# Second last chunk's first MLP products shared between token halves, and the last chunk's inverse placed by VectorE transposes

## The chip, the core and the metric

The kernel runs on one NeuronCore of a Trainium2 chip. The metric is the device time of one execution in microseconds (us). The core has a matrix engine (TensorE, PE in the profile; its weight loads are PEld), a vector engine (VectorE, DVE), an engine for functions and copies (ScalarE, ACT), a general engine (GpSimd, POOL) and a queue that issues most of the transfers (SyncE, SP). Each engine runs its own instructions in the order in which they were written down and waits on semaphores for the others. Products land in PSUM, eight banks of 128 partitions x 512 numbers; everything else lies in SBUF.

## The reference

```python
B, H, S, D = 4, 8, 768, 48                # q, k, v; beta is (B, H, S)
k_n = k / (norm(k) + 1e-6)
state = zeros(B, H, D, D)
for t in range(S):                        # the attention block
    y[:, :, t] = q_t @ state
    v_old = state^T @ k_n_t
    state = state + beta_t * outer(k_n_t, v_t - v_old)
x = y with heads side by side             # 3072 tokens x 384
h = x @ w_in                              # w_in 384 x 2048
out = (h * sigmoid(h)) @ w_out            # w_out 2048 x 384
```

## The kernel before

The sequence of 768 steps is cut into six chunks of 128 (`c` = 0 to 5), each with two halves of 64 steps. With four batches a half has 256 tokens for the MLP.

**Attention.** The recurrence inside a chunk is solved with the inverse of a triangular matrix. For each chunk `prepare` makes the scores of keys and queries (L539), sends the 32 x 32 diagonal blocks to DRAM and back (`block_out`, `block_in`), and `invert` builds their inverse on VectorE: 31 pairs of a rank-one product (L656) and an add (L661), then a scaling (L664). From chunk 2 on the inverse goes from there to DRAM and back (`low`, `up`, `read_up`) to reach the partitions at which the two `merge` steps (L808) want it; chunk 1 instead calls `put_up`, which makes two 32 x 32 block transposes on VectorE and ten copies (six by ScalarE, two by VectorE, two by GpSimd). `solve(c)` then has the merges, the products with keys, values and queries (L854, L866, L886, L932, L945), and for each half the copies of the output into `xT` (L554), part of them by way of DMAs (L925).

**MLP.** The 2048 features are 16 blocks of 128, worked through as eight pairs. For chunks 0 to 4 `hidden(c, hf)` does one half at a time: a pair takes 2 x 3 products of 128 x 256 into one bank `phid` (two banks, called M, in turn), and ScalarE applies `silu` (L1098) into `gT`. For the last chunk `hidden_of_both` (products at L1303) takes both halves at once. It treats two neighbouring pairs as a 2 x 2 block matrix (two feature blocks by two of the three 128-row blocks of `w_in`) times a 2 x 2 block matrix (those rows by two halves) and makes that with seven block products in place of eight; the third block of rows is added plainly. So a group of two pairs takes 22 products in place of 24. The price is sums of blocks of `w_in` and of `xT` (four each, VectorE), copies of intermediate values by ScalarE, and adds by VectorE (L1277). The steps of a group are `first` (6 products), `second` (the rest). `combine(c, hf)` makes the second MLP product in the same manner: 7 x 8 products of 192 columns (L1200) into the banks `px` and `py`, with sums of `gT` on VectorE (L1183) and the results collected in `o` and `kept`.

**Order.** TensorE gets these parts interleaved by hand. A string for each chunk says what comes next: `s` a step of `solve`, `r` the next three or four products of the MLP, `y` a step of `prepare`, `g` the start of an inverse, `i` one pair of its rank steps, `m` norms for a later chunk. Every instruction is pinned behind the one before it on its engine (`pin`), so that the string fixes the order on each of them. PSUM banks are dealt out by name: M (two), A (three), CC (three). A bank is taken again when the last reader of its old content is done.

```python
def bank(room, name):
    tag = room[0]
    room.rotate(-1)
    return kept_banks.get(tag) or banks.tile([P, 512], FP32, name=name, tag=tag)
...
for c in range(1, NCH):
    if c > 1:
        solving = solve(c)
        if c < LAST: pieces = chained(pieces, feed_forward(c, 0), feed_forward(c, 1))
        else:        pieces = chained(pieces, hidden_of_both(c), combine(c, 0), combine(c, 1))
    ready = prepare(c + 1)
    for word in chunks[c].split(): ...
```

Of the kernel before, what the change touches and what calls it, by code (L numbers as in the profile page):

```python
# [19 lines left out]
def kernel(  # L20
# [374 lines left out]
    def norm_steps(c):  # L395
# [25 lines left out]
        if c < 2:  # L421
# [24 lines left out]
    def place(c, j):  # L446

        return 2 * (1 - j % 2) + j // 2 if c > 1 else j
# [181 lines left out]
    def put_up(x):  # L630

        both = work.tile([P, BH, T], FP32, name="xe_y", tag="g", bufs=1)
        xes[1], ys[1] = both[:], both[:].rearrange("p (g h) t -> p g h t", g=2)
        pin(nc.vector.transpose(out=both[:].rearrange("p n s -> p s n"), in_=x))
        up = work.tile([P, BH, T], FP32, name="up_1", tag="x", bufs=1)[:]
        pin(nc.vector.transpose(out=up.rearrange("p n t -> p t n"), in_=x.rearrange("p s t -> p t s")))
        for j in (1, 3, 0, 2):
# [7 lines left out]
    def invert(c, step):  # L645
# [23 lines left out]
        if c == 1:  # L669
            put_up(x)  # L670
# [390 lines left out]

    def hidden_rows(c, hf, fs):

        if (c, hf) in ((0, 1), (LAST, 0)):
            return kq_rows[:, fs]
        if c == LAST:
            i, n = fs.start // (NFF // 4), fs.start % (NFF // 4)
            room = kbufs[i][:].rearrange("p b a e w -> p (b a e w)").rearrange("p (f t) -> p f t", t=2 * GT)
        else:
            room, n = gTs[fs.start // FG], fs.start % FG  # L1070
        return room[:, n : n + fs.stop - fs.start]
# [4 lines left out]
    def groups_of(c):  # L1076

        n = NFF // 4 if c == LAST else FG
        return [slice(f, min(f + n, NFF // 2)) for f in range(0, NFF // 2, n)]

    def hidden(c, hf):

        for f in range(NFF // 2):
            assert ("in", f) in narrowed
            ph = bank(M, "phid")
            for j in range(2):
                for a in range(NKT):
                    pin(nc.tensor.matmul(  # L1088
                        ph[:, j * GT : (j + 1) * GT],
                        lhsT=w_in[:, a, (2 * f + j) * P : (2 * f + j + 1) * P],  # L1090
                        rhs=xTs[c, hf][:, a, :],
                        start=(a == 0), stop=(a == NKT - 1),
                    ))
                if j == 0:
                    yield
            if f % FG == 0 and (c, hf) != (0, 1):
                gTs[f // FG] = mlp.tile([P, FG, 2 * GT], FP32, name="gT", bufs=3)
            pin(nc.scalar.activation(  # L1098
                out=hidden_of(c, hf, f), in_=ph[:], func=ACTF.Silu, scale=-0.5 if in_blocks(c) else 0.5
            ))  # L1100
# [74 lines left out]
    def sum_g(c, hf, which, g):  # L1175
        k, left, right, op = which
        fs = groups_of(c)[g]
# [7 lines left out]
    def combine(c, hf):  # L1185
# [27 lines left out]
        def steps(chain, *halfway):  # L1213
# [7 lines left out]
        gs = range(len(groups_of(c)))  # L1221
        yield from steps(
            chain(px[:, left], (0, 0), (0, 0), True), *((s, g) for g in (gs if last else gs[-1:]) for s in (S1, S2))
# [36 lines left out]

    def hidden_of_both(c):

        free = deque((*M, *CC, *A))
        sums = stage[:, 0 : 3 * NFF // 2 * P].rearrange("p (k f m) -> p k f m", k=3, m=P)
        turns = stage[:, 3 * NFF // 2 * P :].rearrange("p (k t) -> p k t", k=4)

        def of_w(i, k, fs):
            return w_in[:, k].rearrange("p (f i m) -> p f i m", i=2, m=P)[:, fs, i]

        def left(which, fs):  # L1270
            return of_w(*which, fs) if isinstance(which, tuple) else sums[:, which - 1, fs] if which < 4 else of_w(1, 0, fs)

        def right(which):
# [523 lines left out]
```

## Time and profile before

| | |
|---|---|
| median of 3 runs | 632.37 us (631.95 to 634.43) |
| the profiled execution, its own time | 633.96 us |
| its span, first to last instruction | 631.8 us |
| TensorE busy | 617.7 us, 98% of the span |
| VectorE busy | 415.5 us, 66% |
| ScalarE busy | 226.7 us, 36% |
| GpSimd busy | 94.0 us, 15% |
| granted clock of TensorE, mean | 0.989 |

The time of an execution is its span and some 2 us around it. A row of the timeline has the start in us from the span's start, the length, the engine, the line of the kernel, the operation, what it writes and reads, the shapes, and in brackets how long the engine stood idle before and what ended that. Rows of equal instructions are merged (`x12`). The chain of work lists the pieces that ended last, in order of time, with start, length and count; there a product of 128 columns of weights counts twice, since it has two records in the trace.

### The profile page before, as it was taken

To read this page: it belongs to the slowest core of one execution; us is meant where nothing else is said; L and a number is where in the kernel's file an instruction comes from. 1 tells how busy PE (TensorE), PEld (TensorE's weight loads), DVE (VectorE), ACT (ScalarE), POOL (GpSimd) and SP (SyncE) were. 2 spreads that over 40 slices of the span, in tenths; PEclk is the share of its full clock that TensorE was granted. 3 is DMA by queue.
4 is the path that set the end of the run, shared out by engine and by line. 5 is a ranking of instruction groups with operands and counts; after the bars stand their busy time and mean duration, and the time that the engine had idled before them with its cause. 6 is when DMAs were issued, how large, how long until landed. Compare 5 with 4: busy or idle time off the path is not lost.

```text
span 631.8 us, 21374 instructions
## 1 busy us (share of the span) xinstructions
PE 617.7 (98%) x9390; PEld 543.3 (86%) x9390; DVE 415.5 (66%) x927; ACT 226.7 (36%) x516; POOL 94.0 (15%) x101
## 2 busy tenths in 40 slices
PE   8889989999999999999999999999999999999997
PEld 5578778666799989989989989989989989988997
DVE  6886779999667974546975554976444983345432
ACT  4657873332441122451122451122452122454210
POOL 5234631335020020020020010020002000000000
PEclk9869999999999999999999999999999999999999
DMA  9656506350459360459141359433254024010011
GB/s 175 134 141 199 170 16 149 116 86 4 101 100 186 62 108 4 95 107 188 34 92 20 72 125 156 65 75 44 52 113 95 2 75 62 17 38 1 0 26 26
DMA packets 136941, 52.61 MB, mean 83 GB/s; under 512 B 108672, under 2 KB 130432, under 8 KB 136848
## 3 DMA queue, kind: packets, MB, share of 16 engines
q1 hardware_dynamic: 136512, 51.09, 39.6%
q8 instruction: 74, 1.21, 0.9%
q10 hardware_dynamic: 336, 0.15, 0.1%
q14 instruction: 19, 0.16, 0.1%
HBM read 39.09 MB, written 9.96 MB: 78 GB/s over the span
## 4 chain that ended last, share of the span: by engine, by line
PE 93%; SPq 2%; DMA 1%; issue 1%; ACT 1%; DVE 0%
PE phid L1088 34%; PE px L1200 17%; PE py L1200 13%; PE po L1132 5%; PE pb_c L866 3%; PE pa L539 2%; SPq L144 2%; PE pb_c L1303 2%; PE pb_c L854 2%; PE pyc L945 2%; PE pc L1303 2%; PE pb_c L1132 2%; PE pb_c L886 2%; PE pa L1303 1%; PE pyc L932 1%; PE px L808 1%
## 5 line engine op out<-in xcount | busy, mean ns | idle before, releaser
L1088 PE MATMUL phid<-xT,w_in 128*128 128x256 f32 x960 | 214.9, 382 | 1.9 <-issue 1.7
L1088 PEld LDWEIGHTS phid<-xT,w_in 128*128 128x128 f32 x960 | 180.2, 190 | 26.9 <-issue 2.8
L1098 ACT ACTIVATE gT<-phid 128x512 f32<-128x512 f32 x72 | 42.9, 597 | 115.2 <-PE phid L1088 106.2
L656 DVE SCALAR_TENSOR_TENSOR rank<-g,step,x 128x31 f32<-128x31 f32 (+15 forms) x124 | 49.8, 402 | 23.3 <-DMA g<-blocks 19.8
L1200 PE MATMUL px<-sums_of_w,sums_of_g 128*128 128x192 f32 x320 | 56.6, 329 | 0.0
L1200 PE MATMUL py<-w_out,sums_of_g 128*128 128x192 f32 x320 | 56.2, 328 | 0.0
L1200 PEld LDWEIGHTS px<-sums_of_w,sums_of_g 128*128 128x128 f32 x320 | 52.2, 190 | 0.4
L1200 PEld LDWEIGHTS py<-w_out,sums_of_g 128*128 128x128 f32 x320 | 52.3, 190 | 0.3
L661 DVE TENSOR_TENSOR x<-x,rank 128x31 f32<-128x31 f32 (+15 forms) x124 | 42.5, 342 | 4.3
L477 POOL TENSOR_TENSOR vf<-vf,n_slot 128x768 f32<-128x768 f32 x10 | 14.8, 1492 | 175.4 <-DMA vf<-in_v_dram 129.9
L1183 DVE TENSOR_TENSOR sums_of_g<-gT 128x384 f32<-128x384 f32 (+1 forms) x48 | 24.6, 540 | 14.6 <-ACT gT L1098 14.5
L498 DVE STREAM_TRANSPOSE kq<-stage 128x512 f32<-128x512 f32 x28 | 28.4, 1121 | 6.8 <-DMA stage<-in_q_dram 3.5
L554 ACT COPY xT<-pyc 48x128 f32<-48x128 f32 (+2 forms) x120 | 31.1, 259 | 1.6
L1211 DVE TENSOR_TENSOR o<-o,kept 128x192 f32<-128x192 f32 (+1 forms) x29 | 11.5, 425 | 26.7 <-ACT kept L1208 26.7
L560 POOL COPY g<-x 64x256 f32<-64x256 f32 x4 | 5.0, 1244 | 150.8 <-DVE x L664 150.8
L891 DVE TENSOR_TENSOR state<-state,pb_c 128x384 f32<-128x384 f32 x22 | 11.2, 550 | 24.6 <-PE pb_c L886 24.6
L866 PEld LDWEIGHTS pb_c<-vf,xi 64*64 64x64 f32 x736 | 23.3, 138 | 3.2 <-issue 2.3
L866 PE MATMUL pb_c<-vf,xi 64*64 64x48 f32 x736 | 24.9, 223 | 0.1
L1132 PE MATMUL po<-w_out,gT 128*128 128x384 f32 x64 | 23.7, 491 | 0.0
L1200 PE MATMUL py<-w_out,gT 128*128 128x192 f32 x128 | 23.4, 331 | 0.0
L859 DVE TENSOR_TENSOR vf<-vf,pb_c 128x384 f32<-128x384 f32 x22 | 11.2, 550 | 18.3 <-PE pb_c L854 15.5
L1200 PE MATMUL px<-w_out,gT 128*128 128x192 f32 x128 | 22.4, 327 | 0.0
(293 smaller groups left out, 1094.5 us busy)
## 6 DMA issues: line engine op xcount, KB each, us to landing
vf<-in_v_dram SPq DMA_DIRECT2D x48, 96.0 KB, 2.8
out_dram<-o SPq DMA_DIRECT2D x42, 96.0 KB, 2.2
w_out<-in_moe_w_in_dram SPq DMA_DIRECT2D x4, 768.0 KB, 5.0
sums_of_w<-in_moe_w_out_dram SPq DMA_DIRECT2D x4, 768.0 KB, 4.6
kb<-in_k_dram SPq DMA_DIRECT2D x12, 192.0 KB, 4.5
kb<-in_k_dram SPq DMA_DIRECT2D x24, 96.0 KB, 4.0
raw<-in_moe_w_in_dram SPq DMA_DIRECT2D x3, 768.0 KB, 6.8
blocks<-ap SPq DMA_DIRECT2D x32, 64.0 KB, 1.9
```

What stands on the lines that cost most here:

```text
L477: pin(nc.gpsimd.tensor_tensor(out=vf, in0=vf, in1=of, op=ALU.mult))
L498: pin(nc.vector.transpose(out=kqs[c, b][:, :, j, :].rearrange("p a (i m) -> p a m i", i=T), in_=src.rearrange("p a (m d) -> p a m d", d=D) ...
L554: return pin(nc.scalar.copy(to, of))
L656: pin(nc.vector.scalar_tensor_tensor(out=tv, in0=g[:, 0:m, m : m + 1].to_broadcast([P, m, n]), scalar=step[:, m : m + 1], in1=x[:, m : m + ...
L661: yield pin(nc.vector.tensor_tensor(out=x[:, 0:m, m:T], in0=x[:, 0:m, m:T], in1=tv, op=ALU.add))
L866: yield pin(nc.tensor.matmul(pz[rows, n * D : (n + 1) * D], lhsT=xis[g][rows, u * H + 2 * p + e, :], rhs=vfs[c][rows, hf, g * HB + u, p, : ...
L1088: pin(nc.tensor.matmul(ph[:, j * GT : (j + 1) * GT], lhsT=w_in[:, a, (2 * f + j) * P : (2 * f + j + 1) * P], rhs=xTs[c, hf][:, a, :], star ...
L1098: pin(nc.scalar.activation(out=hidden_of(c, hf, f), in_=ph[:], func=ACTF.Silu, scale=-0.5 if in_blocks(c) else 0.5))
L1132: pin(nc.tensor.matmul(pos[i][:, 0:DM], lhsT=hidden_of(0, hf, f // 2)[:, at : at + C], rhs=w_outs[f // HFF][:, f % HFF, :], start=(f == 0) ...
L1183: pin(nc.vector.tensor_tensor(out=sums_of_g[:, k, fs], in0=of[0], in1=of[1], op=op))
L1200: pin(nc.tensor.matmul(to, lhsT=at, rhs=quarter(f, *b) if isinstance(b, tuple) else sums_of_w[b][:, f], start=start and f == 0, stop=f == ...
L1303: pin(nc.tensor.matmul(to[:, i * GT : (i + 1) * GT], lhsT=left(a, slice(f, f + 1))[:, 0], rhs=right(b), start=start and i == 0 and n == 0, ...
```

## The change

In chunk 4 the pairs (0,1), (3,4) and (6,7) are made for both halves at once in the manner of the last chunk; pairs 2 and 5 stay as they were, one half at a time (`plain`). The class `Both` holds the steps of a group, now named one by one: `first` (6 products), `sums`, `second`, `rest`, `third` (2 each), `fourth`, `last` (4 each). `most_of_both(c)` writes out their order; it has four banks, the two of M and one each of A and CC. `others(c)` makes pairs 2 and 5 of the second half between the two `combine` parts. Results of the second half go to free rooms (`kbufs[0]`, `stage`), its sums in `combine` are made in four groups in place of three. The block sums of `w_in` made in chunk 4 are kept, so the last chunk sums only those of pairs 2 and 5, after its third `first`.

For the last chunk `invert` calls `put_up` as chunk 1 does, the ten DMAs by way of DRAM are gone, and the order of the diagonal blocks (`place`) is the plain one, for which GpSimd clears `spread` first. The strings for chunks 4 and 5 are new, with the `i` steps spread over more of chunk 4 and its end in chunk 5.

```diff
+        if c == NCH - 1:
+            pin(nc.gpsimd.memset(spread[:], 0.0))
...
-        return 2 * (1 - j % 2) + j // 2 if c > 1 else j
+        return 2 * (1 - j % 2) + j // 2 if 1 < c < NCH - 1 else j
...
-    def put_up(x):
+    def put_up(c, x):
         both = work.tile([P, BH, T], FP32, name="xe_y", tag="g", bufs=1)
         pin(nc.vector.transpose(out=both[:].rearrange("p n s -> p s n"), in_=x))
+        if c > 1:
+            yield
...
-        if c == 1:
-            put_up(x)
+        if c in (1, NCH - 1):
+            yield from put_up(c, x)
             return
...
+    class Both:
...
+        def first(self, f):
+            self.chain_of[f] = at, a = self.take("pa")
+            yield from self.products(a, f, ((0, 0), (0, 0)), start=True)
+            by_act(self.place(f, 0, 0), halves_of(a))
+            tag, b = self.take("pb")
+            yield from self.products(b, f, ((0, 1), (1, 0)), ((0, 2), (2, 0)), start=True)
+            self.add(self.place(f, 0, 0), b)
+            self.late.append(self.place(f, 0, 0))
+            self.free.append(tag)
+        def begin(self, f):
+            self.p, self.d = ({**getattr(self, at, {}), f: self.take(name)} for at, name in (("p", "pc"), ("d", "pd")))
+        def sums(self, f):
+            p = self.p[f][1]
+            yield from self.products(p, f, (S_1, 1), start=True)
+            by_act(self.place(f, 1, 1), halves_of(p))
+        def second(self, f):
+            a = self.chain_of[f][1]
+            yield from self.products(a, f, (S_2, 2))
+            by_act(self.place(f, 0, 1), halves_of(a))
...
+        def third(self, f):
+            a, to = self.chain_of[f][1], self.place(f, 1, 1)
+            yield from self.products(a, f, (S_3, 3))
+            for of in (a, self.d[f][1]):
+                self.add(to, of)
+            silu(self.c, to, to)
+            self.free.append(self.d.pop(f)[0])
+        def fourth(self, f):
+            to = self.place(f, 0, 1)
+            yield from self.products(self.p[f][1], f, (S_4, (1, 1)), ((0, 2), (2, 1)))
+            self.add(to, self.p[f][1])
+            silu(self.c, to, to)
+            self.free.append(self.p.pop(f)[0])
+        def last(self, f):
+            at, a = self.chain_of.pop(f)
+            yield from self.products(a, f, ((1, 1), 4), ((1, 2), (2, 0)))
+            silu(self.c, self.place(f, 1, 0), halves_of(a))
+            self.free.append(at)
...
+    def most_of_both(c):
+        for f in range(ALONE.start, ALONE.stop, FG):
+            room_for(f // FG)
+            yield from plain(c, 0, f)
+            yield
+        room_for(len(TWOS) - 1)
+        rooms = A.popleft(), CC.popleft()
+        both = Both(c, (*M, *rooms), zbuf[:, 0:HB]...)
+        one, two, three = (fs.start for fs in TWOS)
+        yield from both.first(one)
+        together(both.sum_x(), sum_w_in(TWOS[0]))
+        yield from both.first(two)
+        both.begin(one)
+        yield from both.sums(one)
+        yield from both.second(one)
+        both.outputs()
+        yield from both.rest(one)
+        yield from both.fourth(one)
+        together(sum_w_in(TWOS[1]))
+        yield from both.third(one)
+        both.begin(two)
+        yield from both.sums(two)
+        yield from both.second(two)
+        yield from both.last(one)
+        for which in (S1, S2):
+            sum_g(c, 0, which, 0)
+        yield from both.rest(two)
+        yield from both.fourth(two)
+        together(sum_w_in(TWOS[2]))
+        yield from both.third(two)
+        yield from both.first(three)
+        yield from both.last(two)
+        for which in (S1, S2):
+            sum_g(c, 0, which, 1)
+        both.begin(three)
+        yield from both.sums(three)
+        yield from both.second(three)
+        both.outputs()
+        for step in (both.rest, both.third, both.fourth, both.last):
+            yield from step(three)
...
-        4: "s2 r4 ... y r2 y r6 i r i2 r i2 r i r i r i3 r i r i2 r k i r ... r i r m i2 r m3 r m4 r m4 ... m99",
-        5: "r s r2 s r s r2 s r s r s r s r2 s r s r2 s",
+        4: "s2 r4 ... y r2 y r6 i r i2 r i r i2 r i r i r i r i r i r ... i r i2 r i r i2 r i r i r i r i2 r i r2",
+        5: "r2 s i r2 s r s r2 s r s r s r s r s r s r2 s",
...
-            if c < LAST:
+            if c < LAST - 1:
                 pieces = chained(pieces, feed_forward(c, 0), feed_forward(c, 1))
+            elif c < LAST:
+                pieces = chained(pieces, most_of_both(c), combine(c, 0), others(c), combine(c, 1))
```

More of the change, by code (lines that the diff above doesn't have):

```diff
@@ new lines, in room_for, with plain @@
+    def room_for(i):
+        gTs[i] = mlp.tile([P, FG, 2 * GT], FP32, name="gT", bufs=3)
+    def plain(c, hf, f):
+        assert ("in", f) in narrowed
+        ph = bank(M, "phid")
+        for j in range(2):
+            for a in range(NKT):
+                pin(nc.tensor.matmul(
+                    ph[:, j * GT : (j + 1) * GT],
+                    lhsT=w_in[:, a, (2 * f + j) * P : (2 * f + j + 1) * P],
+                    rhs=xTs[c, hf][:, a, :],
+                    start=(a == 0), stop=(a == NKT - 1),
+                ))
+            if j == 0:
+                yield
+        silu(c, hidden_of(c, hf, f), ph[:])
@@ L1081, in hidden @@
     def hidden(c, hf):
         for f in range(NFF // 2):
[L1084 to L1095, printed above, removed]
@@ L1176, in sum_g @@
         k, left, right, op = which
-        fs = groups_of(c)[g]
+        fs = groups_of(c, hf)[g]
         of = [
@@ L1377, in feed_forward, with others @@
+    def others(c):
+        room_for(0)
+        flush()
+        for f in range(ALONE.start, ALONE.stop, FG):
+            yield from plain(c, 1, f)
+            yield
     def feed_forward(c, hf):
```

199 lines of the change are left out of this document (100 added, 99 removed), and 2 rows, old and new, of the table chunks.

## The prediction

> **What bounds the kernel now.** The page's busy shares and its chain by engine come first.
> ```profile
> PE 617.7 (98%) x9390; PEld 543.3 (86%) x9390; DVE 415.5 (66%) x927; ACT 226.7 (36%) x516; POOL 94.0 (15%) x101
> PE 93%; SPq 2%; DMA 1%; issue 1%; ACT 1%; DVE 0%
> ```
> Next the busy times by stage: from chunk 4's second half to the end of chunk 5's first products.
> ```profile
> 461.56:482.78 21.22, 21.22 (x208) 18.55 (x209) 9.91 (x17) 10.21 (x29) 3.95 (x4) 1.00 0.59 112
> 482.78:500.98 18.20, 18.20 (x113) 18.20 (x112) 14.78 (x39) 2.41 (x6) 0.00 (x0) 1.00 0.06 22
> 500.98:521.70 20.72, 20.72 (x98) 18.24 (x97) 16.89 (x41) 4.51 (x8) 1.25 (x1) 1.00 0.22 58
> 521.70:552.10 30.40, 30.16 (x882) 28.08 (x880) 11.31 (x23) 10.78 (x30) 0.00 (x0) 1.00 0.29 41
> ```
> Columns after the stage and its length: PE, PEld, DVE, ACT, POOL busy (instructions), granted clock, DMA share, GB/s. TensorE is full in every stage that the change touches: a product saved shortens the kernel, and any wait of TensorE, of which there is almost none now, lengthens it. VectorE already fills 14.78 of 18.20 us in the second stage, where the inverse runs.
>
> **1. Saved: 6 products, -2.6 us.** The chain of work gives their price.
> ```profile
> 461.56 4.08 PE phid L1088 x18
> 568.56 3.45 PE pc L1303 x16
> 572.01 1.73 PE pa L1303 x8
> ```
> A product has two records, so 3.45 / 8 = 0.431 us. A group of two feature pairs takes 22 products in place of 24; chunk 4 has three such groups (its pairs 2 and 5, and the last chunk, keep their counts): 6 x 0.431 = 2.59 us. That is 0.41% of the span, so it alone stays within 0.5%, about what a measurement of this kernel can tell from no change. What follows are waits that the new order makes. Instructions of each engine run in the order written, so I take that order from the code and time it by rows of this trace.
>
> **2. First wait: a PSUM bank behind ScalarE's queue, +2.9 us.** `first(0)` comes right after pair 5's last three `phid` products. It puts its `pa` in one M bank and its `pb` in the other, which pair 5's `phid` holds until ScalarE has read it.
> ```profile
> 461.67 1.06 ACT L554 COPY part<-pyc 48x512 f32<-48x512 f32 x2 [2.59 <-PE pyc L945]
> 462.76 3.25 ACT L554 COPY xT<-pyc 48x128 f32<-48x128 f32 x12
> 466.03 1.09 ACT L1098 ACTIVATE gT<-phid 128x512 f32<-128x512 f32 x2
> L1098 ACT ACTIVATE gT<-phid 128x512 f32<-128x512 f32 x72 | 42.9, 597 | 115.2 <-PE phid L1088 106.2
> ```
> That read stands behind fourteen copies of chunk 4's output and begins at 466.03. Before, six more `phid` products (in the other bank) and the scoring products covered it. Now only five products do: TensorE is ready at 461.56 + 5 x 0.431 = 463.72, the bank is free at 466.03 + 0.60 = 466.63. Wait 2.91 us; the saving is gone here already.
>
> **3. Four short waits, +0.9 us.** With only four banks the next group's `pc` reuses a bank that VectorE must empty first, and needs a block sum made after that.
> ```profile
> 559.77 0.42 DVE L1277 TENSOR_TENSOR stage<-xT 128x256 f32<-128x256 f32 x1
> 560.90 0.42 DVE L1277 TENSOR_TENSOR stage<-xT,stage 128x256 f32<-128x256 f32 x1
> 572.05 0.69 DVE L1277 TENSOR_TENSOR kb<-kb,pc 128x512 f32<-128x512 f32 x1 [0.92 <-PE pc L1303]
> 584.21 0.69 DVE L1277 TENSOR_TENSOR kb<-kb,pb_c 128x512 f32<-128x512 f32 x1 [4.03 <-PE pb_c L1303]
> 584.93 0.69 DVE L1277 TENSOR_TENSOR kb<-kb,pd 128x512 f32<-128x512 f32 x1
> 585.53 0.68 DVE L1277 TENSOR_TENSOR kb<-kb,pa 128x512 f32<-128x512 f32 x1
> ```
> An add takes 0.69, starts follow each other by (585.53 - 584.21) / 2 = 0.66; four dependent sums of 256 take 1.5 to the next start. Hand-over from TensorE about 0.1 (0.04 at 572.05). After group 0's `fourth`, VectorE needs 0.1 + 0.66 - 0.05 + 0.42 = 1.13 and 0.1 back, TensorE has two products (0.86): wait 0.35. The same again in the last chunk, whose sums for pairs 2 and 5 now come just ahead of their use: 0.35. The `last` of groups 0 and 1 each wait for the add of `third`, which stands behind the four sums: 0.1 each. Sum 0.9; bounds 0.3 and 1.6.
>
> **4. VectorE falls behind in group 2, +1.65 us.** The order mixes the inverse's rank steps with the adds that release banks.
> ```profile
> 474.81 0.55 DVE L1183 TENSOR_TENSOR sums_of_g<-gT 128x384 f32<-128x384 f32 x1
> 475.39 0.56 DVE L1183 TENSOR_TENSOR sums_of_g<-sums_of_g,gT 128x384 f32<-128x384 f32 x1
> 486.07 0.27 DVE L656 SCALAR_TENSOR_TENSOR rank<-g,step,x 128x31 f32<-128x31 f32 x1 [1.58 <-DMA g<-blocks]
> 492.54 0.45 DVE L656 SCALAR_TENSOR_TENSOR rank<-g,step,x 128x220 f32<-128x220 f32 x1
> 493.02 0.39 DVE L661 TENSOR_TENSOR x<-x,rank 128x220 f32<-128x220 f32 x1
> 493.32 1.35 DVE L1183 TENSOR_TENSOR sums_of_g<-gT 128x384 f32<-128x384 f32 x3
> ```
> From the end of group 1's `fourth` to the end of the first add of group 2's `third`, VectorE has: hand-over 0.1, one add 0.66, four block sums 1.5, nine rank pairs 492.54 - 486.07 = 6.47, three adds 1.98, two sums of the 384 form 1.14, the add itself 0.69: 12.54. At four places an unrelated instruction follows a pair, and starts some 0.12 sooner (493.32 is before 493.02 + 0.39): 12.05. TensorE meanwhile has `third` 2, `first` 6, `last` 4, and of group 2 2 + 2 + 2 + 2 + 4 products: 24 x 0.431 = 10.34, and 0.1 of part 3. Then `last(6)` must wait for that add: 12.05 + 0.05 - 10.44 = 1.65; 0.8 to 2.6 if a start costs 0.05 more or less, or GpSimd slows VectorE:
> ```profile
> 476.26 2.91 POOL L477 TENSOR_TENSOR vf<-vf,n_slot 128x768 f32<-128x768 f32 x2 [53.80 <-DMA vf<-in_v_dram]
> 478.43 1.15 DVE L1183 TENSOR_TENSOR sums_of_g<-gT 128x384 f32<-128x384 f32 x1 [2.48 <-ACT gT L1098]
> ```
> The 1.15 in place of 0.55 fell under a GpSimd multiply; by its own transfer that ends about 479.2, ahead of the stretch above (from about 487). The rank's DMA landed by 486.07; VectorE now comes to it 3.6 us later, so that wait goes and starts nothing sooner.
>
> **5. The combine's first bank, +1.6 us.** `px` takes the bank in which `last(6)` was made. ScalarE must first apply two `silu`s, one of them behind VectorE's add of `fourth(6)`, which stands behind the next rank pair.
> ```profile
> 585.65 0.63 ACT L1321 ACTIVATE kb<-kb 128x512 f32<-128x512 f32 x1 [2.99 <-DVE kb L1277]
> 591.90 0.60 ACT L1321 ACTIVATE kq<-pa 128x512 f32<-128x512 f32 x1 [1.13 <-PE pa L1303]
> ```
> From the start of `last(6)`: add 0.04 + 0.61, pair 493.32 - 492.54 = 0.78, add 0.69, hand-over 0.04, two `silu`s 0.58 + 0.60: 3.34. TensorE has four products, 1.72: wait 1.6. At least 0.8 (its own `silu` and two hand-overs), at most 2.2.
>
> **6. The inverse without DRAM, 0.** The trip was hidden: its pieces are DMAs that nobody waited for.
> ```profile
> 515.64 0.85 DVE L557 COPY g<-x 64x768 f32<-64x768 f32 x1
> 517.00 0.45 SPq L106 DMA_DIRECT2D low<-g  x1
> 526.99 1.29 PE L808 MATMUL py<-xe,ap 32*32 32x32 f32 x128
> 134.93 1.96 DVE L634 STREAM_TRANSPOSE xe_y<-sums_of_w 128x1024 f32<-128x1024 f32 x1
> 139.33 0.62 ACT L554 COPY xi<-up 32x512 f32<-32x512 f32 x1
> 531.08 1.08 PE pb_c L854 x64
> 597.07 2.60 PE py L1200 x16
> ```
> The inverse took 515.6 - 486.07 = 29.5 us; it now starts near 489.7 and takes in some 4.0 of adds, 2.2 of sums and 2.2 of waiting for `kept`: about 527.6, 529.6 with the transpose (1.96, as chunk 1's). The first merge comes at 526.99 + 4.1 (waits up to there, less 2.59) + 4 products of 192 (2.60 / 8 = 0.325): 532.4. Cover 2.8 us. The second merge waits for ScalarE: two copies of `y` and six placements, 1.2 + 6 x 0.62 = 4.9, against twelve products and the keys, 3.9 + 1.1 = 5.0 with switches: just covered; 0 to 0.8 if not. Ten DMAs leave SP's queue, behind which nothing stood. The `spread` memset falls on an idle GpSimd (it idled 53.80 before its multiply), and the extra sums of four groups in `combine(4, 1)` into a stage with 11.31 of 30.40 us of VectorE busy: 0.
>
> **Sum.** -2.59 + 2.91 + 0.9 + 1.65 + 1.6 = +4.5 us. The profiled execution took 633.96 us (span 631.8 and 2.2 around it) and would take 638.5; the median of the runs, 632.37, lies 1.6 below it, so 636.9. With the low bounds of parts 3 to 5 +2.2, with the high ones +6.7: 634.6 to 639.1.
>
> **Rivals.** *The clock falls in the 2.9 us gap (+1.7 us, 638.6).* At the kernel's start a gap of 1.20 us among small products was followed by a granted clock of 0.50:
> ```profile
> 16.72 0.27 PE L539 MATMUL pa<-kq 48*64 48x64 f32 x1 [1.20 <-ACT kq L520]
> 18.00:19.00 1.00, 0.56 (x5) 0.83 0.66 116
> 19.00:20.00 1.00, 1.00 (x4) 0.50 0.61 102
> ...
> 22.00:23.00 1.00, 1.00 (x9) 0.96 1.01 392
> ```
> (the clock stands behind the bracket). With the two rows left out, also at 0.50, that is 0.34 + 3 + 0.08 = 3.4 us at half speed, a cost of 1.7; here the work around the gap is dense, and only the scoring products after it are small. [...] *VectorE keeps up, the other side (-2.59 + 2.91 = +0.3, 632.7).* If the 12.05 us of part 4 took 10.4, parts 3 to 5 would vanish together. It needs every VectorE start 14% sooner than in rows that have no slack; only seams that I count twice speak for it. *The bank is free in time (+1.6, 634.0).* It decides if the read of `phid` came before 463.7, that is ahead of the twelve copies; the order written speaks against. *The placement is late (+5.3, 637.7)*, part 6's second merge. That fewer products are saved cannot be: the count is fixed.
>
> **Chances.** Forecast 0.63, clock 0.12, late placement 0.05, VectorE keeps up 0.11, bank free 0.04, 0.05 for a gain from something unseen. Slower by over 0.5% (beyond 635.5): 0.12 + 0.05 and 0.61 of the forecast, 0.78. Within 0.5%: 0.11 + 0.04 and 0.02 of the forecast's low end, 0.17. Faster by over 0.5%: 0.05. The range, 634.0 to 639.3, takes in the forecast's bounds, the clock and the late placement.
>
> **What would show it.** Right: 12 fewer matmul records; a wait of TensorE of 2.5 to 3 us at the first `pb` behind ScalarE's `gT<-phid`; VectorE without idle time from about 487 to 500; waits of 1 to 2 us at `last(6)` and at the first `px` of `combine(4, 0)`; none at the merges. Wrong: TensorE busy throughout chunk 4, or a granted clock under 1.00 there.

## The result and the profile after

The changed kernel takes 639.84 us (median of 6 runs, 636.88 to 641.75), the kernel before in the same comparison 632.49 us: a ratio of 1.0106, 95% interval 1.0073 to 1.0138. By the ratio that is 6.7 us slower, where 4.5 were forecast. The median lies 0.5 us above the upper end of the forecast range (639.3); 1.0106 times the 632.37 us from which the forecast started is 639.1, just inside. The profiled execution, the longest of the six, has a span of 640.0 us, 8.2 more than before.

The list of TensorE's waits from 455 us to the end (line waited for, us in all, times, longest) shows where it stands still; before, nothing longer than 0.2 us stood there.

```profile
PE pb L1340 <- ACT gT L1106: 2.7, 1, 2.7
PE pa L1340 <- DVE stage L1298: 1.3, 1, 1.3
PE px L1233 <- ACT gT L1106: 1.3, 1, 1.3
PE pb_c L1340 <- DVE gT L1298: 1.1, 1, 1.1
PE pc L1340 <- DVE stage L1298: 0.8, 2, 0.4
```

In order: `pb` of the first group behind ScalarE's queue (part 2), `last` of group 2 (part 4), the combine's `px` (part 5), a wait at `pd` of group 0 that no part named (the list shows its bank as `pb_c`, the name under which the bank is kept), and the two at `pc` (part 3).

The chain of work, last product piece before the change's first wait and last piece of the kernel:

```profile
455.74 4.08 PE phid L1117 x18
633.39 2.61 PE py L1233 x16
```

Before, these stood at 455.67 and 625.67 us, so the stretch between them grew by 7.72 - 0.07 = 7.65 us. The terms, each measured from start to start in the trace:

| | forecast | measured |
|---|---|---|
| six products saved (12 records fewer: 9378 for 9390) | -2.59 | -2.59 |
| part 2, first `pb` | +2.91 | +2.91 |
| rival, clock falls in that gap | (1.7, chance 0.12) | +1.70 |
| wait at `pd` of group 0 | none | +1.33 |
| part 3, four short waits | +0.9 | +1.58 |
| part 4, `last` of group 2 | +1.65 | +1.54 |
| part 5, `px` of the combine | +1.6 | +1.52 |
| part 6, inverse without DRAM | 0 | 0 |
| sum | +4.5 | +8.0 |

(0.3 us of the sum are not found in the 7.65.) A wait costs more than its idle time in brackets: the engine's last product before it is shown 0.17 us longer than the distance of products in a row, and the first pair after it takes about 0.1 more. So 1.27 and 1.25 us of idle time cost 1.54 and 1.52.

**First wait, clock and third wait in one chain.** The timeline of the changed kernel, several engines (start, length, engine, line, operation, in brackets the idle time before and what ended it):

```profile
466.09 0.60 ACT L1106 ACTIVATE gT<-phid 128x512 f32<-128x512 f32 x1
466.74 3.60 PE L1340 MATMUL pb<-xT,w_in 128*128 128x256 f32 x8 [2.75 <-ACT gT L1106]
470.17 0.30 PE L457 MATMUL pg<-pick,spread 128*128 128x32 f32 x2
476.04 3.11 POOL L479 TENSOR_TENSOR vf<-vf,n_slot 128x768 f32<-128x768 f32 x2 [54.06 <-DMA vf<-in_v_dram]
476.12 1.70 DVE L1298 TENSOR_TENSOR z<-xT,z 128x256 f32<-128x256 f32 x1
477.74 1.69 DVE L1298 TENSOR_TENSOR w_in<-w_in 128x256 f32<-128x256 f32 x1
479.36 0.68 DVE L1298 TENSOR_TENSOR gT<-gT,pb_c 128x512 f32<-128x512 f32 x1
480.08 1.13 PE L1340 MATMUL pb_c<-xT,w_in 128*128 128x256 f32 x4 [1.05 <-DVE gT L1298]
```

The silu that frees the bank begins at 466.09 (forecast 466.03) and `pb` at 466.74. Its four products then take 470.17 - 466.74 = 3.43 us, twice the 1.73 of four products at 0.431: half clock. Because of that the scoring, and behind it the eight block sums on VectorE, come 1.7 us later than they would, and the last two of them fall under GpSimd's multiply of `vf`: 1.70 and 1.69 us in place of 0.42. The add that frees the bank of `pd` stands behind them, and TensorE waits for it.

**The clock**, in windows cut at whole multiples of 3.41 us from the first fall at 19.46 us (stretch, length, then busy time of PE, PEld, DVE, ACT, POOL, granted clock, DMA share, GB/s):

```profile
16.05:19.46 3.41, 2.23 (x70) 1.90 (x71) 3.20 (x6) 2.92 (x12) 2.55 (x7) 1.00 0.81 123
19.46:22.88 3.42, 3.42 (x10) 2.16 (x9) 3.01 (x13) 0.17 (x2) 0.00 (x0) 0.50 0.74 159
463.19:466.60 3.41, 0.80 (x4) 0.38 (x2) 2.05 (x3) 3.27 (x13) 0.00 (x0) 1.00 0.19 46
466.60:470.01 3.41, 3.27 (x8) 2.64 (x9) 0.51 (x1) 0.56 (x2) 0.00 (x0) 0.50 0.55 130
```

The clock is 1.00 in the whole of one stretch and 0.50 in the whole of the next. The next fall after 19.46 began at 36.53, 17.07 us or five stretches later, and 466.60 lies 447.14 us behind 19.46, 131 stretches of 3.413 us: the three falls of this execution lie on one grid. The stretch before the fall at 466.60 had TensorE busy for 0.80 of 3.41 us. Before the fall at 19.46, among small products, it was busy for 2.23; among wide ones that much work did not bring a fall (2.14 and 2.16 us in the stretches from 500.74 and 504.15 us of this trace, both followed by 1.00).

**VectorE in group 2**, timeline, and the two waits that it makes:

```profile
501.74 0.68 DVE L1298 TENSOR_TENSOR stage<-stage,pa 128x512 f32<-128x512 f32 x1
502.45 0.69 DVE L1298 TENSOR_TENSOR stage<-stage,pd 128x512 f32<-128x512 f32 x1
502.47 0.70 PE L1340 MATMUL pa<-z,w_in 128*128 128x256 f32 x2 [1.27 <-DVE stage L1298]
503.06 0.44 DVE L665 SCALAR_TENSOR_TENSOR rank<-g,step,x 128x220 f32<-128x220 f32 x1
503.84 0.68 DVE L1298 TENSOR_TENSOR stage<-stage,pb_c 128x512 f32<-128x512 f32 x1
504.55 0.63 ACT L1106 ACTIVATE stage<-stage 128x512 f32<-128x512 f32 x1 [0.75 <-DVE stage L1298]
505.09 0.58 ACT L1106 ACTIVATE gT<-pa 128x512 f32<-128x512 f32 x1
505.72 2.87 PE L1233 MATMUL px<-w_out,gT 128*128 128x192 f32 x16 [1.25 <-ACT gT L1106]
```

`last` starts right when the add of `third` is done; the rank pair at 503.06 delays the add of `fourth`, that the silu at 504.55, that the silu of the bank that `px` takes. This is parts 4 and 5 as they were written down.

**The inverse** (VectorE, and TensorE's first merge in the chain of work):

```profile
528.42 1.22 DVE L673 TENSOR_TENSOR x<-x,step 128x1024 f32<-128x1024 f32 x1
529.68 1.99 DVE L636 STREAM_TRANSPOSE xe_y<-x 128x1024 f32<-128x1024 f32 x1
535.87 1.22 PE py L817 x82
```

It is ready at 529.6 us and transposed at 531.7, 4.2 us ahead of the merge; both come later than the prediction has them (529.6 with the transpose, merge at 532.4). No merge waits.

### The profile page after: what moved, and what is told of

Same layout as the page of the kernel before. It is cut to its first block, busy times and chain, and to the rows that moved or that the text cites. A ratio compares the mean times of both kernels' runs of the same rounds, so it can differ in the third digit from the quotient of the medians.

```text
span 640.0 us, 21398 instructions
## 1 busy us (share of the span) xinstructions
PE 618.1 (97%) x9378; PEld 540.7 (84%) x9378; DVE 429.3 (67%) x958; ACT 235.5 (37%) x531; POOL 94.3 (15%) x103
## 4 chain that ended last, share of the span: by engine, by line
PE 89%; DVE 4%; ACT 3%; issue 1%; DMA 1%; SPq 1%; POOL 0%; DVEq 0%; ACTq 0%; POOLq 0%
PE phid L1117 27%; PE px L1233 17%; PE py L1233 13%; PE po L1165 5%; PE pb_c L875 3%; PE pb_c L1340 2%; PE pa L541 2%; PE pb_c L863 2%; PE pc L1340 2%; PE pa L1340 2%; PE pyc L954 2%; PE pb_c L1165 2%; PE pb_c L895 1%; PE pb L1340 1%; PE pyc L941 1%
## 5 line engine op out<-in xcount | busy, mean ns | idle before, releaser
L1117 PE MATMUL phid<-xT,w_in 128*128 128x256 f32 x816 | 183.5, 382 | 1.0 <-issue 0.7
L1117 PEld LDWEIGHTS phid<-xT,w_in 128*128 128x128 f32 x816 | 152.8, 190 | 22.5 <-issue 2.1
L1106 ACT ACTIVATE gT<-phid 128x512 f32<-128x512 f32 x60 | 35.7, 597 | 93.5 <-PE phid L1117 89.2
L1216 DVE TENSOR_TENSOR sums_of_g<-gT 128x384 f32<-128x384 f32 (+1 forms) x44 | 21.3, 509 | 8.2 <-ACT gT L1106 8.0
L541 PE MATMUL pa<-kq 48*64 48x128 f32 (+1 forms) x384 | 19.9, 255 | 2.3 <-ACT kq L522 1.2
L541 PEld LDWEIGHTS pa<-kq 48*64 48x64 f32 x384 | 18.1, 133 | 4.7 <-ACT kq L522 2.1
L1233 PE MATMUL px<-w_out,gT 128*128 128x192 f32 x116 | 20.7, 328 | 1.3 <-ACT gT L1106 1.3
```

Of the source, the lines that this page charges most:

```text
L541: pin(nc.tensor.matmul(pa[e][half, p * n * W : (p + 1) * n * W], lhsT=kq[rows, p, 0, half], rhs=kq[rows, p, js[0] : js[-1] + 1, half], sta ...
L1106: pin(nc.scalar.activation(out=to, in_=of, func=ACTF.Silu, scale=-0.5 if in_blocks(c) else 0.5))
L1117: pin(nc.tensor.matmul(ph[:, j * GT : (j + 1) * GT], lhsT=w_in[:, a, (2 * f + j) * P : (2 * f + j + 1) * P], rhs=xTs[c, hf][:, a, :], star ...
L1216: pin(nc.vector.tensor_tensor(out=sums_of_g[:, k, fs], in0=of[0], in1=of[1], op=op))
L1233: pin(nc.tensor.matmul(to, lhsT=at, rhs=quarter(f, *b) if isinstance(b, tuple) else sums_of_w[b][:, f], start=start and f == 0, stop=f == ...
```

## Experiments

**1. The gap filled.** The bank wait is left, but TensorE works through it.

```diff
 def first(self, f):
     self.chain_of[f] = at, a = self.take("pa")
+    for _ in range(6 if self.c < LAST and f == 0 else 0):
+        pin(nc.tensor.matmul(a[:, 0:GT], lhsT=..., rhs=self.x((0, 0)), start=True, stop=True, ...))
```

> Six extra products (0.431 us each, 2.59 us) are written into the bank of the first group's pa, just ahead of its own two, which overwrite them; nothing else changes and the result is the same. They lie in the 2.75 us in which TensorE waits for ScalarE to empty the bank of pb. Theory one, the clock fell because of that gap, and the late, slow sums on VectorE under GpSimd's multiply are its consequence: the wait shrinks to about 0.2 us, the granted clock stays at 1.00 through 466 to 470 us, the 1.70 us of half speed go, the block sums come 1.7 us sooner, ahead of GpSimd's multiply at 476.0, and the 1.05 us wait at the first pd goes with them (with its restart about 1.3): 2 to 3 us shorter than the changed kernel, span about 637. Theory two, the clock falls for another reason (the transition itself, or a limit over time): the clock still reads 0.50 for some 3 us and the span stays at 640. Theory three, the sums are slow whatever their time: only 1.7 us are won.

Measured: 638.68 us (10 runs), ratio to before 1.0063 (1.0033 to 1.0094); span of the profiled execution 637.0. Timeline:

```profile
466.86 1.99 PE L1340 MATMUL pb<-xT,w_in 128*128 128x256 f32 x8 [0.17 <-ACT gT L1106]
474.63 0.42 DVE L1298 TENSOR_TENSOR z<-xT,z 128x256 f32<-128x256 f32 x1
474.96 0.42 DVE L1298 TENSOR_TENSOR w_in<-w_in 128x256 f32<-128x256 f32 x1
475.95 2.91 POOL L479 TENSOR_TENSOR vf<-vf,n_slot 128x768 f32<-128x768 f32 x2 [52.30 <-DMA vf<-in_v_dram]
502.91 2.87 PE L1233 MATMUL px<-w_out,gT 128*128 128x192 f32 x16 [1.25 <-ACT gT L1106]
```

The clock stays at 1.00, the two sums take 0.42 each and are done before GpSimd's multiply, and the wait at `pd` is gone. From the last `phid` products (461.67 here, 461.57 in the changed kernel) `px` comes 2.9 us sooner: 1.70 for the clock and 1.2 for the wait. Theory one holds. The span agrees (3.0 us less), and so do the ratios (0.43%, 2.7 us).

**2. The borrowed rooms first.**

```diff
-        both = Both(c, (*M, *rooms), zbuf...)
+        both = Both(c, (*rooms, *M), zbuf...)
```

> The four banks are taken in another order: the two borrowed rooms (one of A, one of CC) first, then the two M banks; nothing else changes. Theory one, the wait at the first pb is only a matter of which bank it takes: pair 5's silu now has ten more products and the scoring to hide it, the 2.75 us wait goes, with it the half clock (1.70) and the 1.05 us wait at the first pd. px of combine then takes an M bank that another group's step emptied earlier, so its 1.25 us wait goes too. The wait at last of group 2 (1.27) stays. Sum about -3.0 - 1.7 - 1.3 - 1.5 = -7.5 us against the changed kernel, some of it (up to 1.5) given back as scoring waits for the banks that are left in A and CC: about 632.5 to 634.5 by the median, near the kernel before. Rival, the banks of A and CC come free no sooner because their readers stand in the same ScalarE queue: the wait moves to pa or to the scoring products and the time stays within 1 us of the changed kernel.

Measured: 634.24 us (10 runs), ratio 1.0013 (0.9988 to 1.0037), span 633.4: with one line 0.93 of the 1.06% are gone, each with an interval of some 0.3 either way. In the traces, from the `phid` products near 455 us to the last product, it is 626.79 - 454.44 = 172.35 us, against 177.65 in the changed kernel and 170.00 before: 5.3 of the 7.65 us. The waits at the first `pb` and at `px` are gone, the scoring waits 0.3, `last` of group 2 still waits 1.3, one `pc` 0.4. One wait is new (timeline):

```profile
475.41 2.90 POOL L479 TENSOR_TENSOR vf<-vf,n_slot 128x768 f32<-128x768 f32 x2 [53.69 <-DMA vf<-in_v_dram]
476.47 0.69 DVE L1298 TENSOR_TENSOR kb<-kb,pb_c 128x512 f32<-128x512 f32 x1 [2.11 <-PE pb_c L1340]
477.07 1.52 DVE L1298 TENSOR_TENSOR stage<-w_in 128x256 f32<-128x256 f32 x1
478.65 1.13 PE L1340 MATMUL pb_c<-z,stage 128*128 128x256 f32 x4 [1.43 <-DVE stage L1298]
```

Everything comes sooner, and now group 1's block sums meet the multiply: 1.52 in place of 0.42. The add just before, one of whose inputs lies in PSUM, takes its usual 0.69 under the same multiply.

**3. The inverse alone.** The kernel before, with `put_up` for the last chunk:

```diff
-        if c == 1:
-            put_up(x)
+        if c in (1, NCH - 1):
+            yield from put_up(c, x)
             return
...
-        4: "... i2 r i r i r m i2 r m3 r m4 ... m99",
+        4: "... i2 r i r i r i2 r5 i r2 i r2 i r",
```

> The kernel before with one part of the change: the last chunk's inverse is placed by VectorE transposes and copies, the ten DMAs are gone; the MLP is as before. Theory one (the prediction's part 6): the trip by DRAM was hidden and the placement is hidden too, no wait at the merges, the time of the kernel before within 0.5 us. Rival: the two transposes and the copies take VectorE and ScalarE 8 us in all and hold up a silu or an add that TensorE waits for: 0.5 to 3 us slower.

Measured: 633.34 us, ratio 0.9999 (0.9972 to 1.0026); no wait at a merge. Part 6 holds: the trip was hidden, and its removal by itself is worth nothing that the interval of 0.27% either way can show. In the traces the time from the combine's product near 425 us to the last product is 624.88 - 425.10 = 199.78 us, against 625.67 - 425.53 = 200.14 before.

**4. The products alone.** The changed kernel with the trip by DRAM:

```diff
...
-        return 2 * (1 - j % 2) + j // 2 if 1 < c < NCH - 1 else j
+        return 2 * (1 - j % 2) + j // 2 if c > 1 else j
...
-        if c in (1, NCH - 1):
+        if c == 1:
             yield from put_up(c, x)
             return
```

> The changed kernel with the other part of the change undone: the inverse goes by way of DRAM again, everything else stays. Theory one: in the new order the scaled inverse is ready at 529.6 us, 14 us later than before; the trip took some 9 us from there to the blocks of the first merge and 12.5 to those of the second, so they land at 538.5 and 542, where TensorE comes at 535.9 and about 541: 2.5 to 3.5 us slower than the changed kernel; the part that is worth nothing by itself is what lets the shared products' order be. Rival: the trip stays hidden, the two kernels agree within 0.5 us.

Measured: 645.82 us (4 runs), ratio 1.0202 (1.0150 to 1.0254), 6.0 us above the changed kernel. Timeline, and windows on this execution's grid:

```profile
539.72 0.25 PE L815 MATMUL py<-xe,ap 32*32 32x32 f32 x4 [2.13 <-DMA xe<-low]
540.87 1.55 PE L815 MATMUL py<-xe,ap 32*32 32x32 f32 x124 [0.90 <-DMA xe<-low]
```

```profile
463.00:466.42 3.42, 1.35 (x7) 0.84 (x5) 1.88 (x3) 3.27 (x13) 0.00 (x0) 1.00 0.23 51
466.42:469.83 3.41, 2.72 (x6) 2.16 (x7) 1.25 (x2) 1.09 (x3) 0.00 (x0) 0.50 0.46 111
469.83:473.24 3.41, 3.41 (x45) 3.15 (x47) 0.00 (x0) 0.30 (x2) 0.00 (x0) 0.50 0.61 123
538.10:541.52 3.42, 0.90 (x80) 0.79 (x82) 0.00 (x0) 0.00 (x0) 0.00 (x0) 1.00 1.07 159
541.52:544.93 3.41, 3.41 (x79) 3.35 (x67) 2.14 (x4) 1.16 (x2) 0.00 (x0) 0.50 1.15 112
```

The first merge waits 3.0 us for `xe`, as theory one said; that wait halves the clock once more (541.52 to 544.93, 1.7 us), and the fall at the first `pb` lasted two stretches here. So in the new order, with the rank steps 14 us later, the removal of the trip is worth some 4.7 us (3.0 and 1.7): it pays for the order of the other part, not for itself. The 6.0 us between the medians are about twice what was expected: the halved clock behind the merge's wait was not foreseen. The second stretch at the first `pb` is some 1.7 us more in this execution, the longest of the four; whether the trip has a part in that, and whether the others had it, no run shows.

**5. Rank steps later**, on top of experiment 2:

```diff
-  4: "... y r6 i r i2 r i r i2 r i r i r i r ... r i2 r i r i2 r i r i r i r i2 r i r2",
+  4: "... y r12 i2 r i2 r i2 r i2 r i2 r i2 r i2 r i2 r i r i r ... r i2 r i r2",
```

> The rooms-first kernel of the second experiment, and the first eight pairs of rank steps of the inverse taken out of the last two groups of shared products; they follow one by one, doubled with the next eight. Theory one (the prediction's part 4): TensorE waits at last of group 2 only because the rank pairs stand ahead of the add that it needs; that wait (1.27 us and its restart, 1.5 in all) goes. Whether the time falls by 1.5 us is the second question. Theory two, VectorE is full from about 486 to 518 us, so work that is postponed comes due before it has room: the doubled pairs hold up the block sums of the first combine and the merges, TensorE waits there 0.8 to 2 us in one to four places, and the whole stays within 0.7 us of the rooms-first kernel. Rival, the 1.27 us wait has another cause (GpSimd, the silu): it stays.

Measured: 634.50 us, ratio 1.0028 (1.0012 to 1.0044), as long as experiment 2 within the two intervals. The wait at `last` of group 2 is gone, and in the first combine there are two new ones:

```profile
511.81 2.84 PE L1233 MATMUL px<-sums_of_w,sums_of_g 128*128 128x192 f32 x16 [0.66 <-DVE sums_of_g L1216]
514.87 1.38 PE L1233 MATMUL py<-w_out,sums_of_g 128*128 128x192 f32 x7 [0.21 <-DVE sums_of_g L1216]
```

Both theories are right at their places: the rank pairs made the wait, and VectorE has no room for eight pairs in a lump 10 us later.

**6. Half the gap filled**, three products in place of six.

> Three extra products in place of six in the gap at the first pb, overwritten as in the first experiment: the gap that is left is 2.75 - 3 x 0.431 = 1.46 us. If a gap of that size among dense products is enough to halve the clock (at the kernel's start 1.20 us was, among small products), the clock reads 0.50 after it as in the changed kernel; if the gap has to be longer, it stays at 1.00 and the later wait at the first pd goes too, span near that of the first experiment.

Measured: one execution, 638.61 us, span 636.8. The gap was 1.47 us, the clock stayed at 1.00 and the wait at `pd` is absent. In this execution the grid cut the gap in two (2.82 and 2.53 of 3.41 us busy), so the run does not show what a gap of this size in one stretch would do.

**7. Every wait treated at its place.**

```diff
-        together(both.sum_x())     
+        together(both.sum_x(), sum_w_in(ALONE))
         yield from both.first(4)
-        together(sum_w_in(ALONE))
...
-        both = Both(c, (*M, *rooms), zbuf...)
+        both = Both(c, (*rooms, *M), zbuf...)
...
         yield from both.first(two)
+        together(sum_w_in(TWOS[1]))
...
-        together(sum_w_in(TWOS[1]))
         yield from both.third(one)
...
-        yield from both.fourth(two)
         together(sum_w_in(TWOS[2]))
+        yield from both.fourth(two)
         yield from both.third(two)
...
-        4: "... s r2 s r3 s2 d v y r3 g ... r6 i r i2 r i r i2 r i r i r i r i r i r ...",
-        5: "r2 s i r2 s r s r2 s r s r s r s r s r s r2 s",
+        4: "... s r2 s r2 s2 r d v y r3 g ... r6 i r i2 r i r i r2 i r i r i3 r i r i r i r i r3 i r i r i r i3 r i r2 i r i r i r i5 r i r2 i r i2 r3 i",
+        5: "r2 s i r2 s2 r2 s r2 s r s r s r s r s r2 s",
```

> The changed kernel with every wait treated at its place: the two borrowed rooms are taken first; one step of products is put ahead of the copies of chunk 4's output; the block sums of pairs 3 and 4 are made right after the second first, ahead of GpSimd's multiply; group 1's third comes before its fourth's sums are needed; the last chunk's block sums come one first sooner; the rank pairs are spread so that none stands ahead of an add that TensorE is about to need. If the waits are all that the change cost, they go (first pb 2.75, pd 1.05, pc 0.41 twice, last 1.27, px 1.25, with their restarts, and the half clock 1.70), and what is left is the saving of six products, 2.59 us: 0.4% below the kernel before, 629 to 631 us by the median; TensorE idle under 0.3 us from 461 us to the end. Rival, the work itself does not fit: VectorE is full from about 486 to 530 us and each wait that is taken away comes back somewhere later, as in the fifth experiment: at or above the kernel before.

Measured: 631.54 us (12 runs), ratio 0.9991 (0.9978 to 1.0005), span of the profiled execution 627.1. That is the time of the kernel before within the interval, not the 629 to 631 us expected. Every wait of the list is gone, and one is new: 0.80 us in the last chunk's second merge (shown below with the tenth). The profiled execution is the shortest of the twelve: from the combine's product to the last product it takes 620.46 - 422.43 = 198.03 us, 2.11 less than the 200.14 before. I took it for ScalarE's placements, the last of which ends at 529.24 us, and tried that.

**8 and 9. The changed kernel again**, two more executions.

> The changed kernel as it is, profiled once more. In the traces so far the half clock starts on a grid of 3.41 us that lies differently in each execution (the first drops began at 18.66, 19.46 and 19.28 us, the later ones whole multiples of 3.41 us behind them), and it followed those stretches of the grid in which TensorE was busy 0.24, 0.26 and 0.40 of the time, not those with 0.50 and more. If that is how it goes, the 2.75 us gap halves the clock where at least some 2.1 us of it fall into one stretch, and not where the grid cuts it nearer to the middle; the span is 640 or 637 us, by that. If the gap itself is the cause, the clock falls every time.

> As the run before it, a third execution of the changed kernel: whether the clock falls at the first pb is expected to follow from where the first drop of this execution (near 19 us) puts the grid of 3.41 us; span 640 us where it falls, 637 where it does not.

Measured: spans 638.1 (time 639.88) and 635.3 (637.05). Windows of the first, on its grid:

```profile
462.16:465.57 3.41, 0.72 (x3) 0.67 (x4) 2.01 (x2) 3.00 (x10) 0.00 (x0) 1.00 0.26 62
465.57:468.98 3.41, 3.41 (x24) 2.87 (x27) 0.00 (x0) 0.19 (x1) 0.00 (x0) 0.50 0.62 141
```

and of the second:

```profile
460.25:463.67 3.42, 2.02 (x10) 1.44 (x8) 2.95 (x4) 3.29 (x12) 0.00 (x0) 1.00 0.43 84
463.67:467.08 3.41, 2.06 (x10) 1.82 (x10) 0.84 (x1) 1.73 (x5) 0.00 (x0) 1.00 0.36 87
```

The same gap of 2.75 us: in the first it falls into one stretch (busy 0.72 of 3.41 us), the clock halves and the wait at `pd` is there; in the second the grid cuts it in two (2.02 and 2.06 busy), the clock stays at 1.00 and the wait at `pd` is absent. (This execution has no fall near 19 us; its grid is taken from its first one, at 33.6 us.) 2.8 us lie between the two spans. Between these two executions it was not the gap that decided, but its place on the grid.

**10. Two placements to GpSimd**, on top of experiment 7.

```diff
-                    by_act(crossed[T * (4 - j) : T * (5 - j)], of)
+                    (by_pool if c > 1 else by_act)(crossed[T * (4 - j) : T * (5 - j)], of)
```

> The kernel of the seventh experiment, whose trace has one wait left in the changed stretch: 0.80 us in the second merge, for the last of six placements that ScalarE makes one after the other (0.62 us each). Two of the six, the copies into crossed, go to GpSimd, which then makes four of 0.63 us and is idle otherwise. Theory (the prediction's rival of the late placement, its mechanism): ScalarE is done 1.24 us sooner, the 0.80 us wait goes, TensorE has no wait above 0.3 us from 461 us to the end, and the kernel is about 1 us shorter than the seventh, 0.3 to 0.5% below the kernel before when executions of like clock are compared. Rival: GpSimd's copies and VectorE's hold each other up (the block sums took 1.52 and 1.69 us under GpSimd's multiply where they take 0.42 alone), the placement is not sooner, and the wait stays.

Measured: 634.19 us, ratio 0.9996 (0.9975 to 1.0016), span 634.6. TensorE in the second merge, and ScalarE's last copies, in the seventh kernel and in the tenth:

```profile
527.37 1.87 ACT L556 COPY xi<-z 32x512 f32<-32x512 f32 x3
529.64 0.21 PE L817 MATMUL px<-crossed,xe_y 32*32 32x32 f32 x1 [0.80 <-issue]
```

```profile
528.91 2.50 ACT L556 COPY xi<-z 32x512 f32<-32x512 f32 x4
534.09 0.26 PE L817 MATMUL px<-crossed,xe_y 32*32 32x32 f32 x1 [1.80 <-issue]
```

My theory fell. The placement was done at 531.4 us, before the wait began (532.3), and the wait was longer: 1.80 us, at the same place, behind the 70th of the merge's 128 products. "issue" says the same: TensorE waited for nothing that the profile shows. Here the clock also halved for two stretches after the wait (0.85 from 520 to 540 us, 0.98 from 540 to 560), behind a stretch of small products with 1.79 us busy.

**11. Products between the small ones**, experiment 7 with the changed kernel's string for chunk 5.

```diff
-        5: "r2 s i r2 s2 r2 s r2 s r s r s r s r s r2 s",
+        5: "r2 s i r2 s r s r2 s r s r s r s r s r s r2 s",
```

> The seventh kernel (placement by ScalarE) with the last chunk's order of the changed kernel again: eight products of 192 columns (2.6 us) stand between the 64 small products of the keys and the 128 of the second merge; in the seventh and tenth kernels the two followed each other directly. The tenth showed the placement done sooner and the wait longer (1.80 us), at the same 70th product of the merge as in the seventh (0.80 us), and put down to nothing that the profile shows. Theory one, TensorE runs short of instructions after some 130 small products in a row (each with its weight load), whatever the data do: the wait goes, none above 0.3 us is left from 461 us to the end, and the kernel is 1 to 1.8 us shorter than the seventh and tenth and 0.3 to 0.5% below the kernel before. Theory two, the wait hangs on data (a placement by VectorE or GpSimd that ends later than its row says): with the merge 2.6 us later it shrinks or goes as well, but the merge then starts late by its data only if the rows of the placement end after it. Rival, it comes at the same place of the merge again: a code position, not the density.

Measured: 631.34 us (12 runs; before in the same comparison 633.12), ratio 0.9969 (0.9946 to 0.9992). Windows:

```profile
461.00:480.00 19.00, 19.00 (x199) 16.17 (x198) 14.12 (x29) 11.65 (x32) 3.96 (x4) 1.00 0.59 115
480.00:500.00 20.00, 20.00 (x100) 17.84 (x99) 16.88 (x42) 7.12 (x13) 0.00 (x0) 1.00 0.10 27
500.00:520.00 20.00, 20.00 (x117) 19.38 (x116) 17.85 (x48) 3.18 (x8) 0.00 (x0) 1.00 0.08 20
520.00:540.00 20.00, 20.00 (x534) 18.75 (x532) 15.27 (x27) 8.68 (x18) 1.21 (x2) 1.00 0.02 4
```

TensorE is full, and the merge waits for nothing. This version is 0.3% shorter than the kernel before, with an interval that just excludes none, and so shorter than the changed kernel: its last product starts 622.96 - 425.17 = 197.79 us after the combine's product at 425.17, against 625.67 - 425.53 = 200.14 before, 2.35 us less, nearly all of the 2.59. Against the seventh kernel's 198.03 us that is only 0.24 less, and the intervals of the two ratios overlap: that the extra order is worth the 1 to 1.8 us expected is not shown. With eight wide products between the 64 small ones of the keys and the 128 of the merge the wait is gone; that TensorE runs short of instructions in a long row of small products fits that, but no row shows it, and a code position that shifted with the string is not excluded. Two things bear on it. Experiment 5 has those eight products too, and TensorE stood still in the second merge there for 0.3 us, with no releaser either. And TensorE stands still in this way near 85 us too, behind a row of small products: 0.68 and 0.96 us in two executions of the changed kernel (in the third, 0.71 us of one stretch there were idle) and 1.71 before. The length of such a stop thus differed between executions of one kernel, and 0.80 against 1.80 us may be no more than that.

## Why the prediction was right, and where its sizes were off

*The bound* (TensorE full, any wait lengthens the kernel) and *the saving* (part 1) hold: experiment 11 gets 2.35 of 2.59 us once the waits are gone.

*Part 2* was right to 0.1 us, and by its mechanism: another bank (experiment 2) removes the wait.

*The clock* was a rival with a chance of 0.12 and was seen in two of three profiled executions of the changed kernel, at the 1.7 us that the rival gave. By the prediction's own list a granted clock under 1.00 in chunk 4 was a sign of being wrong, and on this point it was. The step that failed was to ask whether the work around the gap is dense. Among wide products the fall went with how much of one stretch of 3.41 us was idle: the clock fell after stretches with 0.72, 0.80 and 1.35 us busy at the first `pb`, and not after those with 2.02 and 2.06. Among small products it fell after 2.23 us of them at the start of the changed kernel, 0.90 in experiment 4 and 1.79 in experiment 10.

*Part 3* named four waits and missed the one at `pd`, 1.33 us. It was no error of its own: without the fall of the clock that wait is absent (experiments 1, 6 and 9). The sentence that GpSimd's multiply ends ahead of the sums was right for part 4's stretch and was not asked for group 0's sums. The two waits at `pc` were 0.66 each and not 0.35: 0.1 us of restart was left out at each wait, and VectorE's starts were 0.2 us later than summed.

*Parts 4 and 5* were right to 0.1 us (1.54 for 1.65, 1.52 for 1.6). For part 4 the named cause is shown: in experiment 5 the wait at `last` goes with the rank pairs. For part 5 the bank is (experiment 2 deals out another and the wait is gone); that a rank pair delays it is read from the rows, no run takes that pair away alone. VectorE worked without idle time from 490.6 us on and not from 487, since it waited 2.15 us before 488.80 and 0.65 before 490.60. *Part 6* was right in the order before (experiment 3), and its cover was larger than summed, 4.2 us in place of 2.8.

So the forecast of the mechanism and the sign held; the size was 2.2 us short (4.5 for 6.7), by the clock and by what hung on it. The prediction priced the fall of the clock alone, on top of its middle value (638.6), and not together with the later waits. The time scatters from 636.88 to 641.75 us, and the granted clock with it (0.991 and 0.992 in the two shortest of the six executions, 0.986 to 0.989 in the others); that the grid cuts the gap in some of them and not in others is an estimate from the three profiled ones. The one of these without a fall at the first `pb` took 637.05, near the 636.9 forecast for that case. That nearness is in part luck: the kernel before took 631.85 in that comparison, so the execution was 5.2 us longer, and its terms in the table add up to 5.0.

## What to carry to other kernels

When a saving is spent on waits, look at the place of each wait before giving up the idea: one line that deals out banks in another order returned most of the loss here, and the rest went with the order of small vector instructions around the adds that free banks (changed together in experiment 7, so not priced one by one). In this kernel a gap of TensorE was dearer than its length: 0.3 us more for stopping and starting (1.27 us of idle time cost 1.54), and, where 2.1 to 2.7 us of one 3.41 us stretch fell idle among wide products, 1.7 us more for the clock, and then whatever the delay ran into. A part that is worth nothing alone, as the inverse without DRAM, can be what makes room for another: try each alone and both.

## What the runs showed of the hardware

- The clock changed on a grid of 3.41 us that lay differently in each execution (first fall at 19.46, 18.43 and 33.59 us in the three of the changed kernel); the stretch at half speed at the first `pb` cost 1.7 us. In experiments 4 and 10 the clock took two stretches to recover, though TensorE was busy for 2.72 of 3.41 us in the first (experiment 4). Wide products with 2.02 us busy in a stretch kept the clock (experiment 9), and with 1.35 (experiment 4) they did not; small products lost it after 2.23 us (start of the changed kernel) and after 1.79 (the wait of 1.80 us in experiment 10).
- Under a GpSimd multiply of two SBUF operands, VectorE adds of two SBUF operands took 1.52 (experiment 2), 1.69 and 1.70 us (the changed kernel) in place of 0.42; an add with a PSUM operand kept its 0.69 (experiment 2).
- After some 130 small products in a row TensorE stood still for 0.80 (experiment 7) and 1.80 us (experiment 10) at the same product of a merge, with no releaser in the profile; with eight wide products in between the stop was 0.3 us (experiment 5) or absent (experiment 11). A stop of the same kind near 85 us had 0.68 (the changed kernel) to 1.72 us (experiment 11). The cause is open.
